# Modulation products: 32 equal moving columns in place of dummy matmuls between their chunks

## The chip, the cores and the metric

The kernel runs on one core of one Trainium2 chip, in one launch. The metric is device microseconds of a run. A core has five engines that run side by side and wait for one another through semaphores: TensorE (PE, matmuls; PEld are its weight loads), VectorE (DVE), ScalarE (ACT), GpSimd (POOL) and SyncE (SP, which issues most of the DMAs).

## The reference

A transformer block for 2048 tokens of width 512, with adaptive layer norm. A condition vector `c` gives six vectors of 512 values, which shift, scale and gate the two halves of the block; all tensors are bfloat16.

```
mod = silu(c) @ w_mod                      # (1, 512) @ (512, 6*512)
sa, ca, ga, sb, cb, gb = six slices of mod
h = layernorm(x) * (1 + ca) + sa
x = x + ga * attention(h)                  # 32 query heads, 8 key/value heads of 128,
                                           # the last 512 cached positions, softmax, wo
h = layernorm(x) * (1 + cb) + sb
x = x + gb * (relu(h @ w1) @ w2)           # 512 -> 1792 -> 512
```

## The kernel before

The program is written as one list of operations for each engine, in the order in which the Python code calls `kb.op`. Every engine runs its list strictly in that order; `kb.op` works out from the declared reads and writes which semaphores each operation waits for. So the order of the calls is the order on the engine, and nothing is reordered later.

The 2048 tokens are cut into 4 blocks of 512 (`QB`), and a block into 4 tiles of 128. Block and head make a unit; there are 128 units. For a unit the kernel computes Q (`q_mms`, 4 matmuls of 512 columns), the scores (`s_mms`, 4 of 512), their exponentials on ScalarE, the product with V (`pv_mms`, 16 of 129) and, spread between units as background work, the output projection. The two layers of the feed-forward part stand at the end. In that long stretch TensorE's queue is full.

The change lies ahead of the first unit, in the start of the kernel, where several short chains have to meet:

- **Loads.** `x` of block 0 comes in two DMAs; then `c`; then the first two slices of `w_mod`, which hold `sa` and `ca`, in four DMAs, one for each chunk of 128 input rows (`load_wm01`, chunks 0 and 2 issued by ScalarE, 1 and 3 by SyncE); then the first heads of `wq`, and K and V.
- **The condition vector.** It is transposed by TensorE (line 1418), and ScalarE and VectorE make `silu(c)` of it, in bfloat16, as `sc_bf` (line 1425), one column for each chunk.
- **The modulation products** (`mod_cols_mm`). `sa` and `ca` are wanted with the feature in the partition. So the weights are the stationary operand: for each of 4 chunks `cc`, 2 slices and 4 groups of 128 features, one matmul with 128x128 weights and one moving column `sc_bf[:, cc]`. These 32 matmuls add up eight columns in one PSUM bank (`psQ`). Each chunk waits for its own DMA. `mod_cols_evac` (line 1440, VectorE) then adds 0 or 1 and writes `modc`.
- **The layer norm of block 0.** VectorE makes the statistics of tiles 0 to 2 (`ln_stat`) and normalises them (`ln_norm`, line 1395); ScalarE does tile 3. TensorE transposes each tile in four 128x128 pieces (`ln_tposes`, line 1377). Tiles 0 and 1 go into banks of `psS`, tiles 2 and 3 into banks of `psO` and `psW`.
- **The modulated input.** VectorE and ScalarE scale and shift the transposes with `modc` into `hT` (`mod_half`, lines 1641 and 1643), in two halves of 256 tokens. Then Q of the first heads follows (`q_half`).

`warm(n)` puts n dummy matmuls into TensorE's list: 512 columns of ones against weights of ones, into a PSUM bank whose content nobody reads. They stand in several places of the start: ten at the very beginning, three and two behind statistics of tiles, one between each two chunks' modulation products, three behind the transposes of tiles 0 and 1, and one behind those of tiles 2 and 3. All matmuls go through `mm`, so line 1374 is that of nearly every one; in the profile they are told apart by their operands: `psW<-ones`, `psO<-ones` and `psS<-ones` are dummies, `psQ<-sc_bf,wmw` are the modulation products, `psS<-ident,xn` and `psO<-ident,xn` the transposes.

VectorE's list in that stretch reads: statistics of tile 2, normalisation of tiles 0 and 1, the addition of `mod_cols_evac`, normalisation of tile 2, `mod_half` for two chunks of the first half, then the second half.

Of the kernel before, what the change touches and what calls it, by code (L numbers as in the profile page):

```python
# [9 lines left out]
ALU = mybir.AluOpType  # L10
# [127 lines left out]
def build_general(nc, es, A_x, A_k_cache, A_v_cache, A_wq, A_wo, B_x, B_w1, B_w2, c, w_mod, out, cfg=None):  # L138
# [27 lines left out]

    NQT = cfg.get("NQT", 4)
    NPB = cfg.get("NPB", 4)
# [11 lines left out]
    if True:  # L180
# [4 lines left out]
        def AL(name, n):  # L185
            lay[name] = (off[0], n)
            off[0] += n + (n % 2)
# [8 lines left out]
        AL("U", max(DC * 6 * D + G * KC * Dh, NOT * QB))  # L196
        AL("qT", NQT * QB)
        AL("Pb", NPB * pslot)
# [36 lines left out]
        def ring(name, n, sz):  # L235
            o = lay[name][0]
            return [arena[:, o + i * sz: o + (i + 1) * sz] for i in range(n)]
# [22 lines left out]
        oT = [arena[:, Ub + i * QB: Ub + (i + 1) * QB] for i in range(NOT)]  # L260
        qT = ring("qT", NQT, QB)
        Pb = ring("Pb", NPB, pslot)
# [66 lines left out]
        R_w2 = RL("w2", FC)  # L329
        R_qT = RL("qT", NQT)  # L330
        R_Pb = RL("Pb", NPB)
# [497 lines left out]
        def rec_qp(i, k):  # L829
# [11 lines left out]
            if k == DC - 1:  # L841
                qs = i % NQT
                if LN1_FOLD:
# [6 lines left out]
        def rec_qk(i, tl):  # L850
            b, h = units[i]
            g = h // R
            qs = i % NQT
            pbs = i % NPB
# [344 lines left out]
def build_fast(nc, es, top, A_x, A_k_cache, A_v_cache, A_wq, A_wo, B_x, B_w1, B_w2, c, w_mod, out, flag):  # L1199
    P = 128  # L1200
# [11 lines left out]
    DC = D // P  # L1212
# [10 lines left out]
    NPT = 3  # L1223
    NOS = 4
    NQT = 3
    VW = P + 8

    def T(name, shape, dt=BF):
        return es.enter_context(nc.sbuf_tensor(name, shape, dt))
# [6 lines left out]
    kT_sb = T("kT", [P, G, W])  # L1236
    v_sb = T("v", [P, G, KC, VW])
    hT = [T(f"hT{i}", [P, DC, QB]) for i in range(2)]
# [8 lines left out]
    wm = [wm01[:, :, 0:D], wm01[:, :, D:2 * D]] + [wmw[:, i * DC * D:(i + 1) * DC * D].rearrange("p (c n) -> p c n", c=DC) for i in range(2, 6)]  # L1247
# [12 lines left out]
    m01 = T("m01", [P, 2 * DC], F32)  # L1260
    sc_bf = T("sc_bf", [P, DC])
    sc_f = T("sc_f", [P, DC], F32)
    tmp = T("tmp", [P, DC], F32)
    modc = T("modc", [P, 4 * DC], F32)
# [17 lines left out]
    bank = [s_ps[0][:, 0, :], s_ps[0][:, 1, :], s_ps[1][:, 0, :], s_ps[1][:, 1, :], q_ps[:, :],  # L1282
            o_ps[:, 0:2, :].rearrange("p a b -> p (a b)"), o_ps[:, 2:4, :].rearrange("p a b -> p (a b)"), w_ps[:, :]]
# [3 lines left out]
    kb = KB(nc)  # L1287
    PE = kb.stream("pe", sem("s_pe"))
    ACT = kb.stream("act", sem("s_act"))
    DVE = kb.stream("dve", sem("s_dve"))  # L1290
# [22 lines left out]
    R_b = RL("bank", 8)  # L1313
# [9 lines left out]
    R_cf, R_m01 = Res("cf"), Res("m01")  # L1323
# [32 lines left out]
    def wm_res(sl, cc):  # L1356
        return R_wmc[cc] if sl < 2 else R_wm[sl]
# [15 lines left out]
    def mm(out_ap, lhsT, rhs, start, stop, reads, bk, signal):  # L1373
        kb.op(PE, lambda e: e.matmul(out_ap, lhsT, rhs, start=start, stop=stop), reads=reads, group_writes=[R_b[k] for k in bk], signal=signal)  # L1374
# [4 lines left out]
    def warm(n, gate=(), bk=7):  # L1379
        for i in range(n):  # L1380
            mm(bank[bk], ones[:, :], ones[:, 0:1].to_broadcast([P, QB]), True, True, [R_ones] + list(gate), [bk], i == n - 1)
# [25 lines left out]
    def ln_tposes(tl, bks):  # L1407
        for cc in range(DC):
            bk = bks[cc]
            o = TO[tl // 2][cc] + tl % 2 * P  # L1410
            tpose(bank[bk].bitcast(BF)[:, o:o + P], xn[:, tl, cc * P:(cc + 1) * P], [R_xn[tl]], [bk], cc == DC - 1)
# [15 lines left out]
    def mod_cols_mm(which, bk):  # L1427
        fs = []
        for cc in range(DC):
            for sl in (0, 1):  # L1430
                for c2 in range(DC):
                    last = sl == 1 and c2 == DC - 1 and cc == DC - 1
                    fs.append(lambda sl=sl, c2=c2, cc=cc, col=sl * DC + c2, last=last: mm(
                        bank[bk][:, col:col + 1], wm[sl][:, cc, c2 * P:(c2 + 1) * P], sc_bf[:, cc:cc + 1],
                        cc == 0 and sl == 0 and c2 == 0, last, [R_sc, wm_res(sl, cc)], [bk], last))
        return fs

    def mod_cols_evac(which, bk):
        mo, r = which * 2 * DC, (R_moda, R_modb)[which]
        kb.op(DVE, lambda e: e.tensor_tensor(modc[:, mo:mo + 2 * DC], bank[bk][:, :2 * DC], m01[:, :], op=ALU.add), reads=[R_b[bk], R_m01], writes=[r])  # L1440

    def mod_part(sl, cc):
        dst, r = pr[sl - 2], R_pr[sl - 2]
# [135 lines left out]
    kb.op(POOL, lambda e: e.memset(cst[:, 3:4], -1.0), writes=[R_eps])  # L1579
    kb.op(POOL, lambda e: e.memset(v_sb[:, :, :, P:VW], 1.0), writes=[R_v1])  # L1580
    kb.op(POOL, lambda e: e.memset(m01[:, 0:DC], 0.0), writes=[R_m01])
# [13 lines left out]
    def rstd_pow(lo, hi):  # L1595
# [12 lines left out]
          reads=[R_x[t3], R_nmr, R_rstd[t3]], writes=[R_xn[t3]])  # L1608
# [8 lines left out]
    def q_evac_half(u, hf, bk, eng):  # L1617
# [4 lines left out]
        else:  # L1622
            kb.op(ACT, lambda e: e.activation(dst, src, ACTF.Copy), reads=[R_b[bk]], writes=w)

    fs = mod_cols_mm(0, QBK)
    for i, f in enumerate(fs):
        f()
        if i in (7, 15, 23):
            warm(1, bk=6)
    ln_tposes(0, TB[0])  # L1630
    mod_cols_evac(0, QBK)
    HB = QB // 2
    R_half = [R_h0, R_hT[0]]
# [56 lines left out]
    for g in range(G):  # L1690
        for i, op in enumerate((ALU.max, ALU.min)):
            add((3, 5, 12, 16, 20, 24, 28, 32)[g], lambda g=g, i=i, op=op: kb.op(DVE, lambda e: e.tensor_reduce(vmax[:, i, g:g + 1], v_sb[:, g, :, 0:Dh], axis=AX.XY, op=op),
                                                             reads=[R_v[g]], writes=[R_vmax]))
# [139 lines left out]
def bass_adaLN_cond__sliding_block_cached__dense_activation_relu__prompt_kernel(  # L1833
# [14 lines left out]
    with ExitStack() as top:  # L1848
        flag = top.enter_context(nc.sbuf_tensor("flag", [1, 8], mybir.dt.int32))
        with ExitStack() as es:  # L1850
            kb, fast, cut, dma_cnt, flag_ev = build_fast(nc, es, top, *args, flag)
            sems = dict(kb.sems)
            meet = top.enter_context(nc.semaphore("s_meet"))
# [84 lines left out]
```

## Time and profile before

| | |
|---|---|
| median of 3 runs | 563.0 us (562.88 to 563.35) |
| the profiled execution's own time | 563.35 us |
| its span, first to last instruction | 558.9 us |
| TensorE busy, share of the span | 550.6 us, 99% |
| ScalarE busy | 349.7 us, 63% |
| VectorE busy | 255.0 us, 46% |
| first modulation product starts | 7.21 us |
| first transpose of `xn` starts | 8.66 us |
| first Q product starts | 10.42 us |

All times in the profile are microseconds from the start of the span. A row of the timeline gives the start, the time from the start of the first to the end of the last instruction merged into it, the engine, the line, the operation, the tiles (written, then read), the shape and the count. Matmuls are pipelined: a row's length includes the time until its last result is out, so the pitch, the distance between starts, tells what a matmul costs in a row of others. The ends of matmuls are modelled.

### The profile page before, as it was taken

To read this page: it belongs to the slowest core of one execution; us is meant where nothing else is said; L and a number is where in the kernel's file an instruction comes from. 1 tells how busy PE (TensorE), PEld (TensorE's weight loads), DVE (VectorE), ACT (ScalarE), POOL (GpSimd) and SP (SyncE) were. 2 spreads that over 40 slices of the span, in tenths; PEclk is the share of its full clock that TensorE was granted. 3 is DMA by queue.
4 is the path that set the end of the run, shared out by engine and by line. 5 is a ranking of instruction groups with operands and counts; after the bars stand their busy time and mean duration, and the time that the engine had idled before them with its cause. 6 is when DMAs were issued, how large, how long until landed. Compare 5 with 4: busy or idle time off the path is not lost.

```text
span 558.9 us, 9695 instructions
## 1 busy us (share of the span) xinstructions
PE 550.6 (99%) x4070; PEld 317.1 (57%) x4144; DVE 255.0 (46%) x556; ACT 349.7 (63%) x455; POOL 52.7 (9%) x50
## 2 busy tenths in 40 slices
PE   9999999999999999999999999999999999999997
PEld 4665555555555555555555555555555554444444
DVE  5555555553546544335445443333354438322134
ACT  5986666666666666666666666666666644432500
POOL 2000022004500000033000000332000000000000
PEclk9999999999999999999999999999999999999999
DMA  9998772522224244253453321121123210200001
GB/s 250 283 197 187 131 153 56 114 44 72 38 42 72 39 85 105 60 130 58 97 94 56 76 40 39 39 38 39 38 39 76 39 29 0 50 28 21 21 29 48
DMA packets 113356, 42.66 MB, mean 76 GB/s; under 512 B 93976, under 2 KB 112152, under 8 KB 113304
## 3 DMA queue, kind: packets, MB, share of 16 engines
q1 hardware_dynamic: 112584, 41.08, 36.2%
q10 hardware_dynamic: 720, 0.89, 0.5%
q8 instruction: 33, 0.54, 0.4%
q14 instruction: 19, 0.16, 0.1%
HBM read 18.35 MB, written 2.10 MB: 37 GB/s over the span
## 4 chain that ended last, share of the span: by engine, by line
PE 99%; issue 1%; DVE 0%
PE psS L1374 29%; PE psO L1374 27%; PE psQ L1374 23%; PE psW L1374 20%; PE psS L1377 0%; PE psO L1377 0%; DVE PT L1755 0%; DVE PT L1757 0%; DVE ones L1574 0%; PE psO L1418 0%; PE psW L1377 0%
## 5 line engine op out<-in xcount | busy, mean ns | idle before, releaser
L1498 ACT ACTIVATE PT<-psS 128x1024 bf16<-128x1024 f32 x254 | 260.6, 1028 | 127.0 <-PE psS L1374 126.9
L1374 PE MATMUL psS<-qT,kT 128*128 128x512 bf16 (+1 forms) x514 | 151.4, 377 | 0.2
L1374 PEld LDWEIGHTS psO<-v,PT 128*128 128x128 bf16 x2048 | 126.6, 98 | 30.2
L1374 PE MATMUL psO<-v,PT 128*128 128x129 bf16 x2048 | 137.0, 220 | 0.0
L1374 PE MATMUL psQ<-hT,wq 128*128 128x512 bf16 (+1 forms) x505 | 129.2, 377 | 0.2
L1508 DVE RECIPROCAL rinv<-psO 128x4 f32<-128x4 f32 x128 | 23.4, 183 | 225.2 <-PE psO L1374 225.2
L1374 PE MATMUL psW<-wo,oT 128*128 128x512 bf16 x452 | 118.1, 379 | 3.2
L1509 DVE TENSOR_TENSOR o<-psO,rinv 128x512 bf16<-128x512 f32 x128 | 88.5, 691 | 4.7 <-DVE rinv L1508 0.3
L1374 PEld LDWEIGHTS psS<-qT,kT 128*128 128x128 bf16 x516 | 50.0, 98 | 58.7 <-issue 0.4
L1374 PEld LDWEIGHTS psQ<-hT,wq 128*128 128x128 bf16 x508 | 49.7, 98 | 59.0
L1490 ACT ACTIVATE qT<-psQ 128x512 bf16<-128x512 f32 x125 | 74.0, 592 | 0.0
L1744 ACT ACTIVATE wq<-psS 128x512 bf16<-128x512 f32 x56 | 33.4, 597 | 49.1 <-PE psS L1374 49.1
L1374 PEld LDWEIGHTS psW<-wo,oT 128*128 128x128 bf16 x512 | 44.9, 98 | 32.9 <-DVE acc L1531 1.2
L1531 DVE TENSOR_TENSOR acc<-psW,acc 128x512 f32<-128x512 f32 x48 | 33.2, 691 | 6.7 <-PE psW L1374 6.7
L1374 PE MATMUL psO<-wmw,wq 128*128 128x512 bf16 (+1 forms) x165 | 32.8, 352 | 0.2
L1534 POOL TENSOR_TENSOR acc<-acc,gaf 128x512 f32<-128x512 f32 x12 | 15.6, 1300 | 146.7 <-DVE acc L1531 139.8
L1390 POOL TENSOR_TENSOR rstd<-rstd,cst 128x4 f32<-128x4 f32 x7 | 7.2, 1026 | 217.1 <-DVE rstd L1389 217.1
L1755 DVE TENSOR_TENSOR PT<-psO,gbf 128x512 f32<-128x512 f32 (+1 forms) x12 | 7.5, 624 | 40.4 <-PE psO L1374 40.4
L1374 PE MATMUL psS<-h2T,wmw 128*128 128x512 bf16 x110 | 25.2, 379 | 0.1
L1374 PEld LDWEIGHTS psO<-wmw,wq 128*128 128x128 bf16 x168 | 15.4, 98 | 16.5
L1374 PE MATMUL psS<-hT,wmw 128*128 128x512 bf16 x110 | 24.4, 379 | 0.1
L1384 DVE BATCH_NORM_STATS2 st<-x 128x6 f32<-128x512 bf16 x31 | 21.1, 681 | 3.6 <-DMA x<-in_A_x_dram 3.6
(95 smaller groups left out, 199.3 us busy)
## 6 DMA issues: line engine op xcount, KB each, us to landing
wo<-in_A_wo_dram SPq DMA_DIRECT2D x4, 1024.0 KB, 5.9
wq<-in_A_wq_dram SPq DMA_DIRECT2D x7, 512.0 KB, 5.2
wmw<-in_B_w_dram SPq DMA_DIRECT2D x14, 256.0 KB, 3.0
wmw<-in_w_mod_dram SPq DMA_DIRECT2D x4, 512.0 KB, 4.9
oT<-o SPq DMA_TRANSPOSE x128, 2.4
out_dram<-PT SPq DMA_DIRECT2D x15, 128.0 KB, 1.7
x<-in_A_x_dram SPq DMA_DIRECT2D x3, 512.0 KB, 4.2
v<-in_A_v_cache_dram SPq DMA_DIRECT2D x8, 128.0 KB, 4.7
```

The source lines that it names most:

```text
L1374: kb.op(PE, lambda e: e.matmul(out_ap, lhsT, rhs, start=start, stop=stop), reads=reads, group_writes=[R_b[k] for k in bk], signal=signal)
L1384: kb.op(DVE, lambda e: e.bn_stats(st[:, t, :], x_sb[:, t, :]), reads=[R_x[t]], writes=[R_st[t]])
L1390: kb.op(POOL, lambda e: e.tensor_tensor(rstd[:, sl], rstd[:, sl], cst[:, 0:1].to_broadcast([P, hi - lo]), op=ALU.pow), reads=R_rstd[sl] + ...
L1490: kb.op(ACT, lambda e: e.activation(qT[u % NQT][:, :], bank[bk], ACTF.Copy), reads=[R_b[bk]], writes=[R_qT[u % NQT]])
L1498: kb.op(ACT, lambda e: e.activation(PT[u % NPT][:, pr * 2:pr * 2 + 2, :], s_ps[pr][:, :, :], ACTF.Exp, scale=scale), reads=[R_b[pr * 2], R ...
L1508: kb.op(DVE, lambda e: e.reciprocal(rinv[:, u, :], o_ps[:, :, P]), reads=[R_b[5], R_b[6]], writes=[R_rinv])
L1509: kb.op(DVE, lambda e: e.tensor_tensor(o_sb[u % NOS][:, :, :], o_ps[:, :, 0:P], rinv[:, u, :].unsqueeze(2).to_broadcast([P, TPB, P]), op=A ...
L1531: kb.op(DVE, lambda e: e.tensor_tensor(acc[:, tl, :], bank[WBK], acc[:, tl, :], op=ALU.add), reads=[R_b[WBK], R_acc[tl]], writes=[R_acc[tl]])
L1534: kb.op(eng, lambda e: e.tensor_tensor(acc[:, tl, :], acc[:, tl, :], gaf[:, :], op=ALU.mult), reads=[R_acc[tl], R_ga], writes=[R_acc[tl]])
L1744: kb.op(ACT, lambda e: e.activation(h1T[b % 2][:, fc, :], bank[bk], ACTF.Relu), reads=[R_b[bk]], writes=[R_h1[b % 2][fc]], pre=all_events( ...
L1755: kb.op(DVE, lambda e: e.tensor_tensor(yt[i][:, c0:c1], bank[bk][:, c0:c1], gbf[:, c0:c1], op=ALU.mult), reads=[R_b[bk], R_gb], writes=[R_ ...
```

## The change

The modulation products get a moving operand of 32 columns, all equal: the one column of `silu(c)` is read 32 times through a broadcast. Each product then writes 32 equal columns of PSUM, so the eight results lie 32 columns apart, and `mod_cols_evac` reads the first column of each group. The three dummy matmuls between the chunks are taken out. The dummies in the other places stay as they are, three behind the transposes of tiles 0 and 1 and one behind those of tiles 2 and 3. TensorE's list is shorter by these three matmuls and their weight loads; the other engines have the same instructions in the same order.

```diff
+    NR = 32
...
                     fs.append(lambda sl=sl, c2=c2, cc=cc, col=sl * DC + c2, last=last: mm(
-                        bank[bk][:, col:col + 1], wm[sl][:, cc, c2 * P:(c2 + 1) * P], sc_bf[:, cc:cc + 1],
+                        bank[bk][:, col * NR:(col + 1) * NR], wm[sl][:, cc, c2 * P:(c2 + 1) * P], sc_bf[:, cc:cc + 1].to_broadcast([P, NR]),
                         cc == 0 and sl == 0 and c2 == 0, last, [R_sc, wm_res(sl, cc)], [bk], last))
...
     def mod_cols_evac(which, bk):
-        kb.op(DVE, lambda e: e.tensor_tensor(modc[:, mo:mo + 2 * DC], bank[bk][:, :2 * DC], m01[:, :], op=ALU.add), reads=[R_b[bk], R_m01], writes=[r])
+        kb.op(DVE, lambda e: e.tensor_tensor(modc[:, mo:mo + 2 * DC], bank[bk][:, :2 * DC * NR].rearrange("p (c r) -> p c r", r=NR)[:, :, 0], m01[:, :], op=ALU.add), reads=[R_b[bk], R_m01], writes=[r])
...
     fs = mod_cols_mm(0, QBK)
-    for i, f in enumerate(fs):
+    for f in fs:
         f()
-        if i in (7, 15, 23):
-            warm(1, bk=6)
     ln_tposes(0, TB[0])
     mod_cols_evac(0, QBK)
```

## The prediction

> **What bounds the kernel now.** I read the page first, then the chain that ended last, then the first 12 us engine by engine. The page's sections 1 and 4:
>
> ```profile
> PE 550.6 (99%) x4070; PEld 317.1 (57%) x4144; DVE 255.0 (46%) x556; ACT 349.7 (63%) x455; POOL 52.7 (9%) x50
> PE 99%; issue 1%; DVE 0%
> ```
>
> The chain that sets the end is TensorE from start to finish. The waits of TensorE's matmul row hold one entry in the whole execution, 1.1 us before the first matmul. So a microsecond saved or lost on TensorE's path in the first 10 us arrives whole at the end, and nothing later absorbs it. The edit touches only 7.2 to 8.8 us. The chain in order of time, 0 to 20 us, shows that stretch (start, length, what):
>
> ```profile
> 5.67 1.70 PE psW L1374 x5
> 7.37 0.18 PE psQ L1374 x8
> 7.55 0.24 PE psO L1374
> 7.79 0.18 PE psQ L1374 x8
> 7.97 0.24 PE psO L1374
> 8.21 0.18 PE psQ L1374 x8
> 8.38 0.24 PE psO L1374
> 8.62 0.18 PE psQ L1374 x8
> 8.80 0.47 PE psS L1377 x8
> ```
>
> The psQ rows are the modulation products, the psO rows the three dummies that go, psS the transposes. (The chain counts by ends; the timeline's starts lie 0.16 us earlier.) Read alone, it promises 3 x 0.24 = 0.72 us. What the dummies cover has to be read from the weight loads, from VectorE and from the DMAs. Timeline of the weight loads, then of VectorE:
>
> ```profile
> 7.41 0.46 PEld L1374 LDWEIGHTS psQ<-sc_bf,wmw 128*128 128x128 bf16 x8
> 8.02 0.27 PEld L1374 LDWEIGHTS psQ<-sc_bf,wmw 128*128 128x128 bf16 x8
> 8.27 0.45 PEld L1374 LDWEIGHTS psQ<-sc_bf,wmw 128*128 128x128 bf16 x8
> ```
>
> ```profile
> 7.99 0.73 DVE L1395 TENSOR_SCALAR xn<-x,mv,rstd 128x512 bf16<-128x512 bf16 x2
> 8.84 0.17 DVE L1440 TENSOR_TENSOR modc<-psQ,m 128x8 f32<-128x8 f32 x1
> 8.92 0.40 DVE L1395 TENSOR_SCALAR xn<-x,mv,rstd 128x512 bf16<-128x512 bf16 x1
> 9.31 0.41 DVE L1641 TENSOR_SCALAR hT<-psS,modc 128x256 bf16<-128x256 bf16 x1
> ```
>
> And the DMA view, in a window of 0.16 us around the issues of the third and fourth chunk of the modulation weight (queue, size, us to landing):
>
> ```profile
> wmw<-in_w_mod_dram ACTq DMA_DIRECT2D x1, 256.0 KB, 6.3
> wmw<-in_w_mod_dram SPq DMA_DIRECT2D x1, 256.0 KB, 6.2
> ```
>
> By the timeline these two were issued at 1.72 and 2.06 us, so chunk 2 landed at about 8.0 and chunk 3 at 8.2. The same view gives chunk 0 as issued at 1.24 and 4.2 us to landing, chunk 1 as 1.66 and 5.5: landed at 5.4 and 7.1. The weight loads of chunks 2 and 3 start at 8.02 and 8.27, right behind their landings. The dummies at 7.83 and 8.25 (timeline) thus stand largely in time in which TensorE would have waited for its weights.
>
> **The change part by part.** *Three dummies out.* Each has a pitch of 0.21 us (7.41 to 7.63, 7.83 to 8.04, 8.25 to 8.46), 0.64 us in all, and that is the most this part can give. *32 columns for one in 32 products.* The one-column row has a pitch of 25 ns (eight from 7.21 to 7.41). The transposes, 128 columns each, run at 56 ns (8.66 to 8.72, 8.72 to 8.77), a 512-column dummy at 216 ns (6.99 to 7.21). The line through the last two gives 0.417 ns a column and 2.7 ns fixed, hence 16 ns for 32 columns, below the 25 ns row. So 25 ns it is, the nearest row in length; the other end is 56 ns.
>
> With 25 ns, chunk 0 runs 7.21 to 7.41, chunk 1 (landed at 7.1) 7.41 to 7.61. Then TensorE waits for chunk 2: 8.04 to 8.24, and for chunk 3: 8.29 to 8.49. Before, the products ended at 8.66. So 0.17 us remain of 0.64; the DMAs take the rest. Behind the waiting products in TensorE's queue stand the transposes. Those of tile 0 need its normalised rows, done at about 8.40 (7.99 plus 0.41), so they go at 8.49. Those of tile 1 need rows that VectorE ends at 8.72 (7.99 plus 0.73). Weight loads followed their releaser by 0.06 us elsewhere (sc_bf ends at 7.06, load at 7.12), so load at 8.78 and first transpose near 8.80, against 8.88 before. That is 0.08 us, and it is what the path gains: after them come three dummies, the transposes of tiles 2 and 3, one dummy and the first Q products, back to back from 9.10 to 10.42, and each moves up by as much. The next releasers do not object: the addition on line 1440 goes from 8.84 to about 8.67, the normalisation of tile 2 behind it to 8.75, ending at 9.15, and its transposes are due at 9.68.
>
> *The strided read on line 1440.* Eight values, 32 columns apart, in place of eight adjacent ones: 0.17 us if the count sets it (the one row; its neighbours of 1 to 8 values take 0.15 to 0.18), 0.42 if the 256 columns spanned did (the 256-column read of line 1621). I take 0.17. With 0.42 the normalisation of tile 2 would end at 9.40, still before 9.68; the first scaling of hT on line 1641 would start 0.1 us later, its cover being the 10.42 start of Q.
>
> Nothing else moves. Order on the other engines is unchanged; no DMA is issued elsewhere; in place of the dummies TensorE gets the exposed wait for chunk 2, 0.41 us.
>
> *What the array is fed.* [...] The page's PEclk says 9 in every slice, also the first, so the clock must be read from pitches. From 1.10 to 6.47 the 512-column dummies come 0.43 us apart, then 0.30, then 0.22: half speed until about 6.6 us and full speed ever since. [...] From 6.77 to 10.42 us the array was fed 9 dummies x 512 + 16 transposes x 128 + 32 = 6,688 columns, at 0.42 ns 2.8 of 3.65 us, 77%. Afterwards it is 6 x 512 + 2,048 + 1,024 = 6,144 columns, 2.6 of 3.57 us, 72%. In the products' own stretch it falls from 0.66 of 1.45 us (45%) to 0.43 of 1.28 (34%), with a hole of 0.41 us in it. [...]
>
> [...]
>
> The sum: -0.08 us, between -0.17 (tile 1 no limit) and, at 56 ns a product, 4 x 0.45 us from 7.21 = 9.01, so +0.35. This execution took 563.35 us: a span of 558.9 and 4.45 around it. It would become 563.27; the median of the runs, 563.0, lies 0.35 below, so 562.9. The gain is 0.01%; a measurement of this kernel can tell about 0.2%, 1.1 us, from no change.
>
> **The rivals.** [...]
>
> *The products are the path (faster).* If the landings come earlier in most executions and VectorE's rows too, the 0.64 us come through: 562.35, still within 0.2%. The weight loads at 8.02 and 8.27 speak against it. Nothing in the profile offers the 1.1 us that a measurable gain needs; I leave it what the trace may not show, such as a profiled execution with landings unlike the others'.
>
> *A 32-column product costs as much as a 128-column one.* Then +0.35: 563.35, also within 0.2%. The edit would not do what it says, being dearer than the dummies it replaces. The line through the longer rows speaks against it.
>
> **How the numbers follow.** No change to be measured: 0.51, made up of the forecast (0.36), the products as path (0.07) and the dear products (0.08); its own range is 562.3 to 563.7 with the runs' scatter (562.88 to 563.35). Clock falls: 0.41, most of it between 564.1 and 564.9; above that lies 0.11. Faster by over 0.2%: 0.08. The likeliest case gives 562.9. The range runs from 562.3 to 564.9, leaving out the faster case and the long half-speed stretches, about 2 in 10.
>
> **What would show it.** Right: no dummy rows between the psQ rows; psQ at 25 ns; weight loads of chunks 2 and 3 again near 8.0 and 8.25; the transposes of tile 1 near 8.80; Q's first product near 10.34; pitches of 216 ns for 512 columns all through. Wrong in the clock: pitches of 0.43 us for 512 columns, or 0.21 for 256, somewhere after 8 us. Wrong in the size: psQ at 56 ns, or weight loads of chunk 2 well before 8.0.

## The result, and the profile after

The changed kernel takes 560.97 us (median of 6 runs, 560.93 to 561.68), the kernel before 563.04 (562.88 to 563.56): a ratio of 0.9965, with a 95% interval of 0.9953 to 0.9978. It is 2.1 us faster, outside the predicted range of 562.3 to 564.9.

The profiled execution does not show these 2 us. Its span is 558.7 us, 0.2 below that of before. Page of the changed kernel, head and sections 1 and 4:

```profile
span 558.7 us, 9689 instructions
PE 549.4 (98%) x4067; PEld 316.4 (57%) x4141; DVE 255.1 (46%) x556; ACT 349.7 (63%) x455; POOL 52.8 (9%) x50
PE 97%; issue 1%; DVE 1%; DMA 1%
```

The chain in order of time now leaves TensorE ahead of the transposes: their releaser is VectorE's normalisation (xn), as TensorE was through with the products by then.

```profile
8.08 0.33 DVE xn L1396
8.41 0.05 issue
8.46 0.72 PE psS L1378 x8
```

Weight loads, VectorE, and the first Q products, from the timeline:

```profile
7.12 0.99 PEld L1375 LDWEIGHTS psQ<-sc_bf,wmw 128*128 128x128 bf16 x32 [0.57 <-DVE sc_bf L1426]
8.64 0.16 DVE L1441 TENSOR_TENSOR modc<-psQ,m 128x8 f32<-128x8 f32 x1
8.84 0.41 DVE L1396 TENSOR_SCALAR xn<-x,mv,rstd 128x512 bf16<-128x512 bf16 x1
10.33 0.60 PE L1375 MATMUL psQ<-hT,wq 128*128 128x256 bf16 x4
```

The 32 products run almost in one piece. The first Q product starts at 10.33, 0.09 us before the 10.42 of the kernel before; the span is 0.2 us shorter. Neither difference between these two executions is clear of the scatter: in eight profiled executions of what the kernel before executes (its own and those of the experiments below), the first Q product starts anywhere from 10.02 to 11.08 us. The landings of chunks 2 and 3 (DMA view around their issues) were earlier than in the other execution:

```profile
wmw<-in_w_mod_dram ACTq DMA_DIRECT2D x1, 256.0 KB, 5.9
wmw<-in_w_mod_dram SPq DMA_DIRECT2D x1, 256.0 KB, 5.7
```

Where, then, are the 2 us? In the table of before stood two numbers side by side: the execution's own time, 563.35, and its span, 558.9. Between them lie 4.45 us. In the profiled execution of the changed kernel it is 561.68 and 558.7: 2.98. (It is the slowest of the six; their median outside the span is 2.3.) By definition no instruction is recorded behind the span, but DMAs are. The DMA view from 557 to 565 us, in 40 slices of 0.2 us; first the kernel before:

```profile
GB/s 8 12 6 13 149 3 0 0 0 0 82 0 0 0 0 0 0 0 0 0 0 0 0 0 0 0 0 0 0 0 41 0 0 0 0 0 0 0 0 0
q8 instruction: 1, 0.02, 1.1%
q14 instruction: 1, 0.01, 0.4%
```

and the changed kernel:

```profile
GB/s 12 6 20 142 1 0 0 0 0 82 0 0 0 0 0 0 41 0 0 0 0 0 41 0 0 0 0 0 0 0 0 0 0 0 0 0 0 0 0 0
q8 instruction: 1, 0.02, 1.0%
q14 instruction: 2, 0.02, 0.7%
```

The profile names the kind of queues 8 and 14 "instruction"; I read their transfers as fetches of program code. A slice with 82 GB/s holds one of 16,384 bytes (queue 8), one with 41 GB/s one of 8,192 (queue 14). Both kernels fetch 16 KB in the slices at 559.0 and 558.8, just behind the span. But the last 8 KB start at 563.0 before and at 561.4 after. This fits engines that still have code to run when the span is over, and that took longer over it before the change. The fetch of 8 KB is no exact mark of the end, though: in the run with two matmuls fewer below it lies in the slice from 560.2 to 560.4, and that execution still took 561.61 us.

By its amount I take queue 8 for TensorE's: section 3 of the page before gives it 0.54 MB in 33 fetches, for 8,214 recorded TensorE instructions. That is about 66 bytes each, some 250 instructions to a fetch; I count with 256, an estimate. The three dummies with their weight loads are six instructions, and the heads of the pages differ by six (9695 and 9689). Behind TensorE's last matmul the program jumps over the fallback path (a second version of the whole kernel, run only if a flag says so) to the code that ends it. The jump is a row of the profile of before:

```profile
L1878 PEldq COMPARE_BRANCH  x2: 90/1878/3666, 509.9 to 554.6; - x2
```

Of the two branches on this line, the first, at 509.9, takes 0.09 us; the second, at 554.6, is the jump. It takes 3.67 us, until 558.3, and queue 8 fetches 16 KB during it. In the changed kernel it takes 3.55 us. So the jump itself is hardly different and lies inside the span; but by this estimate six instructions fewer move the end code to another place in a block of fetched code.

### The profile page after: what moved, and what is told of

Same layout as the page of the kernel before. It is cut to its first block, busy times and chain, and to the rows that moved or that the text cites. A ratio compares the mean times of both kernels' runs of the same rounds, so it can differ in the third digit from the quotient of the medians.

```text
span 558.7 us, 9689 instructions
## 1 busy us (share of the span) xinstructions
PE 549.4 (98%) x4067; PEld 316.4 (57%) x4141; DVE 255.1 (46%) x556; ACT 349.7 (63%) x455; POOL 52.8 (9%) x50
## 4 chain that ended last, share of the span: by engine, by line
PE 97%; issue 1%; DVE 1%; DMA 1%
PE psS L1375 29%; PE psO L1375 27%; PE psQ L1375 22%; PE psW L1375 19%; DMA x<-in_A_x_dram 1%; DVE st L1385 0%; PE psS L1378 0%; DVE mv L1386 0%; PE psO L1378 0%; DVE xn L1396 0%; DVE rstd L1594 0%; DVE PT L1754 0%; DVE PT L1756 0%; DVE tmp L1425 0%; DVE sc_bf L1426 0%
```

## The experiments

Theory A: the time hangs on where TensorE's end code lies, hence on the length of its program, not on what the edit does at 7 to 9 us. Rival B: the executed edit brings it. The fallback is never executed for these inputs, so its length can be changed without any effect on the executed instructions. The first two runs use this edit with 3 and with -3:

```diff
+def resize(stream, n):        # n matmuls more, or fewer, in the middle of the fallback
+    ...
                 def rerun():
...
+                    if name == "pe":
+                        resize(general[name], FALLBACK)
                     gkb.emit(general[name], e)
```

**The changed kernel at the old length** (`FALLBACK = 3`).

> The changed kernel, with three matmuls more in the fallback path of TensorE's program, which is not executed for these inputs. TensorE's program is then as long as that of the kernel before; what is executed is that of the changed kernel. Theory A (the 2 us lie outside the span and hang on the length of TensorE's program): span 558.7 us, time back at about 563.0 us. Rival B (the executed edit itself brings the 2 us): span 558.7, time stays at about 561.0 us.

Measured: 563.14 us (ratio 0.9999, 0.9989 to 1.0009), median span 559.0, outside it 4.15. The gain is gone, with the whole edit in place.

**The kernel before at the new length** (`FALLBACK = -3`).

> The kernel before, with three matmuls fewer in the fallback path of TensorE's program, which is not executed for these inputs (the fallback thus lacks three matmuls). TensorE's program is then as long as that of the changed kernel; what is executed is that of the kernel before. Theory A: span 558.9 us as before, time down to about 561.1 us. Rival B: time stays at about 563.0 us.

Measured: 561.51 us (0.9968, 0.9955 to 0.9980), span 558.75, outside 2.7. Most of the gain, with nothing of the edit. Rival B falls with these two.

**32 columns, dummies kept.**

```diff
-                        bank[bk][:, col:col + 1], wm[sl][:, cc, c2 * P:(c2 + 1) * P], sc_bf[:, cc:cc + 1],
+                        bank[bk][:, col * NR:(col + 1) * NR], wm[sl][:, cc, c2 * P:(c2 + 1) * P], sc_bf[:, cc:cc + 1].to_broadcast([P, NR]),
```

(and the strided read on line 1440)

> The kernel before with 32 equal moving columns, the three dummies between the chunks kept. TensorE's program is as long as before. Theory A: 563.0 us, span within 0.1 us of 558.9. Rival B, if the 32 columns bring it: about 561 us.

Measured: 563.13 us (0.9999, 0.9990 to 1.0009). The columns bring nothing and cost nothing that can be measured.

**No dummies, one column.**

```diff
-    for i, f in enumerate(fs):
+    for f in fs:
         f()
-        if i in (7, 15, 23):
-            warm(1, bk=6)
```

> The kernel before without the three dummies, products with one moving column. TensorE's program is as long as that of the changed kernel. Theory A: about 561.0 us, span 558.8, if the clock holds; if the array, fed 5,152 instead of 6,688 columns between 6.8 and 10.4 us, loses full speed, the span grows by about 1.4 us and the time is about 562.4 us. Rival B, if the dummies bring it: 561 us as well; this run tells the columns from the dummies only together with the first two.

Measured: 561.40 us (0.9965, 0.9950 to 0.9979), span 559.0, outside 2.4. The time is that of the shorter program. This run is also the one in which the array is fed least between 6.8 and 10.4 us. Timeline:

```profile
7.48 1.40 PE L1374 MATMUL psQ<-sc_bf,wmw 128*128 128x1 bf16 x32
8.74 0.61 PE L1377 MATMUL psS<-ident,xn 128*128 128x128 bf16 x8
10.50 0.60 PE L1374 MATMUL psQ<-hT,wq 128*128 128x256 bf16 x4
```

Eight transposes in 0.61 us and four matmuls of 256 columns in 0.60 us, as in the kernel before from 8.66 and from 10.42 us on: no speed was lost, after 1.2 us that held nothing but one-column products.

**One and two matmuls fewer** (the kernel before, `FALLBACK = -1` and `-2`).

> The kernel before with one matmul fewer in the unexecuted fallback path of TensorE's program (the fallback lacks it). Theory A, refined: TensorE's last instructions, behind the fallback, straddle the edge of a block of fetched program, and the time outside the span (about 4.2 us before, about 2.4 after the change) goes by steps with their place. Each matmul is two instructions. Either 563.0 us (edge not yet passed) or 561.2 us (passed); nothing in between. Rival (the tail shrinks in proportion to the program's length): about 562.4 us.

> As the run before it, two matmuls fewer. Theory A: 563.0 or 561.2 us, and 561.2 if one fewer gave 561.2. Rival (proportion): about 561.8 us.

Measured: 562.45 us (0.9989, 0.9978 to 0.9999) and 561.73 (0.9980, 0.9970 to 0.9991), outside the span 3.4 and 2.9. These are the rival's numbers, not mine: there is no single step, but between this length and six instructions fewer 0.1 to 0.4 us for each instruction.

**192 and 256 instructions more** (the changed kernel; fulfilled waits behind the fallback, counted as two to an instruction, which no run shows).

```diff
                     gkb.emit(general[name], e)
+                    if name == "pe":
+                        for _ in range(384):      # 512 in the second
+                            e.wait_ge(meet, 1)
```

> The changed kernel with 192 instructions more behind the fallback path of TensorE's program, semaphore waits that are fulfilled at once and are not executed for these inputs. The fetches of TensorE's queue have 16,384 bytes; if an instruction has 64 bytes, that is 256 instructions, and 192 more have the same place in a block as 64 fewer. Theory A: the end code lies wholly inside one block, the time is 561.0 us or less, down to about 559.5 if the second fetch behind the span is not waited for any more. Rival (length in itself): 563 us or more.

> As the run before it with 256 instructions, one whole block. Theory A: same place in the block, same time as the changed kernel, 561.0 us. Rival (length in itself): 563 us or more.

Measured with 192: 560.65 us (0.9959, 0.9945 to 0.9974), outside 1.8. With a longer program the kernel is faster, so length as such is not it. With 256: 561.82 us (0.9982, 0.9972 to 0.9993), outside 3.1. It comes down most of the way, but not to the 2.3 of the changed kernel; it lies where two to four instructions fewer than before lie. The repeat after 256 is thus not exact by my count. Whether the added waits take a few places more than counted, or the block is not quite what I take it for, stays open.

The DMA view of the run with 192, 557 to 565 us, shows the end closer behind the fetch:

```profile
GB/s 14 154 19 3 0 0 0 0 0 0 82 0 0 0 0 0 41 0 0 0 0 0 0 0 0 0 0 0 0 0 0 0 0 0 0 0 0 0 0 0
```

The 16 KB are fetched at 559.0 as before, but the execution ends soon behind them: it took 560.51 us, whereas the kernel before needed almost three more. So that fetch alone is not what costs the time.

**4, 16 and 186 instructions more** (the kernel before, the same edit with 8, 32 and 372 waits).

> The kernel before with 4 instructions more behind the fallback. Theory A: four more instructions of the end code fall behind the edge. If these still belong to what follows the span, the time rises by 4 x 0.3 to about 564.2 us; if they belong to the barrier that ends the span, the second fetch is waited for inside the span, which grows by up to 1.4 us, and the time outside falls by as much: 563.0 us. Rival (before is the worst place by chance, the next step up is a new block): 561 us.

> The kernel before with 16 instructions more behind the unexecuted fallback of TensorE's program (fulfilled semaphore waits). Theory A, as the runs so far leave it: behind the span TensorE needs a second fetch of 16 KB, done near 560.3 us, and what is left of its end code behind the edge of that block costs about 0.3 us an instruction (2.8 us before, 1.5 with six instructions fewer, 0.1 with the end code wholly inside a block). Pushed 16 places on, the end code lies wholly behind the edge, in the block that the jump itself fetches: about 560.7 us. Rival (a longer program costs in proportion, 0.3 us an instruction): about 567 us; a milder rival (the edge only moves into the barrier): 563 us or more.

> The kernel before, executed stream and all, with 186 instructions more behind the fallback: the same place in the block as the changed kernel with 192 more, which took 560.65 us. Theory A: 560.7 us, with the three dummies and the one-column products in place. Rival B (part of that time is owed to the executed edit): 561 us or more.

Measured: 560.49 us (0.9963, 0.9948 to 0.9978), 560.70 (0.9971, 0.9958 to 0.9984) and 560.73 (0.9963, 0.9951 to 0.9975), outside the span 1.8 each. The last two are as theory A had it. The first is a miss: of the three cases the rival's came true. The kernel before stands, by chance, on nearly the worst place, and four instructions further it is over.

**The jump taken away.** TensorE's fallback goes ahead of its last part, as on the other engines, so that no jump lies behind the last matmul.

```diff
-                if name == "pe":
-                    with e.If(v == 128):
-                        last_part()
-                    with e.Else():
-                        rerun()
-                else:
-                    with e.If(v != 128):
-                        rerun()
-                    with e.Else():
-                        last_part()
+                with e.If(v != 128):
+                    rerun()
+                with e.Else():
+                    last_part()
```

> The kernel before with TensorE's two paths in the other order, the fallback first and the last part behind it, so that no jump stands between the last matmul and the end code; the jump now stands in front of the last part, in the feed-forward stretch. Theory A: the time outside the span falls from 4.1 us to 1.8 or less; the span grows by what TensorE loses at the jump, between 0 (if its queue holds enough matmuls) and about 2 us. Time 560.7 to 562.7 us. Rival (the jump is not the cause): time outside the span stays at 4.1 us.

Measured: 560.68 us (0.9965, 0.9950 to 0.9980), span 558.7, outside 2.0. The DMA view, 557 to 565 us:

```profile
GB/s 0 0 90 75 0 0 0 0 0 0 0 0 0 0 0 0 41 0 0 0 0 0 0 0 0 0 0 0 0 0 0 0 0 0 0 0 0 0 0 0
q14 instruction: 1, 0.01, 0.3%
```

Queue 8 fetches nothing behind the span any more. The jump, now in the feed-forward stretch, takes as long as at the end, 3.54 us, but most of it is covered. First its row and the timeline of TensorE there in this run, then the timeline in the kernel before:

```profile
L1877 PEldq COMPARE_BRANCH  x1: 3540/3540/3540, 509.8 to 509.8; - x1
507.07 6.21 PE L1374 MATMUL psO<-wmw,wq 128*128 128x512 bf16 x27
513.40 2.98 PE L1374 MATMUL psQ<-wmw,wq 128*128 128x512 bf16 x13
513.40 2.49 PEld L1374 LDWEIGHTS psQ<-wmw,wq 128*128 128x128 bf16 x13 [0.62 <-issue]
```

```profile
507.15 6.21 PE L1374 MATMUL psO<-wmw,wq 128*128 128x512 bf16 x27
513.20 3.18 PE L1374 MATMUL psQ<-wmw,wq 128*128 128x512 bf16 x14
```

From the first psO to the first psQ it is 6.33 us instead of 6.05, so TensorE loses 0.28 us at the jump. The span hardly shows it (a median of 558.7, with 558.5 of the kernel before in the same set of runs): in the profiled execution the last three output DMAs land 1.5 to 1.6 us after their issue, in that of before 2.0 to 2.8; why, no run here separates. The edit only changes the order of the two paths, so the end code should stand where it stood in the kernel before.

All runs by the length of TensorE's program, in instructions against the kernel before by my count (medians; "outside" is the time less the span of the same run; the kernel before, measured anew with each set of runs, took 563.07, 562.99 and 562.63 us, with 4.25, 4.1 and 4.1 outside):

| TensorE's program | kernels | outside the span, us | time, us |
|---|---|---|---|
| +250 | the changed one | 3.1 | 561.82 |
| +186 | before; the changed one (+192 to itself) | 1.8; 1.8 | 560.73; 560.65 |
| +16 | before | 1.8 | 560.70 |
| +4 | before | 1.8 | 560.49 |
| 0 | before; the changed one; columns only | 4.25; 4.15; 4.0 | 563.07; 563.14; 563.13 |
| -2 | before | 3.4 | 562.45 |
| -4 | before | 2.9 | 561.73 |
| -6 | the changed one; before; no dummies | 2.3; 2.7; 2.4 | 560.97; 561.51; 561.40 |
| no jump | before | 2.0 | 560.68 |

Within one row the times agree within their intervals, whatever the kernel does between 7 and 9 us. Six kernels stand at 560.5 to 561.0, four of them without the edit. So the versions that beat both kernels are those at +4, +16 and +186 and the one without the jump; against the changed kernel they gain 0.2 to 0.5 us at most, which their intervals do not separate.

What is shown: that the number of instructions in TensorE's program decides, though neither more nor fewer is better in itself, and not what is executed; and that at the length of the kernel before the long end goes with the jump over the fallback. Without the jump this one length alone was run. What is argued, and shown by no run: that it is the place in a block of fetched code. The jump does not tell good lengths from bad ones: it takes 3.4 to 3.8 us in all 13 kernels that end with it, 3.67 in the kernel before and 3.73 with four instructions more. And a fetch of 16 KB behind the span is there with 4.25 us outside as with 1.8. The code that runs behind the span is not in the profile, so why an instruction there costs 0.1 to 0.4 us stays open, as does the repeat after 256.

## Why the prediction was wrong

**The step that failed** is the last one of the sum, "a span of 558.9 and 4.45 around it. It would become 563.27", with "Nothing else moves" ahead of it. I held the 4.45 us for a constant. It went to 2.98 in the profiled execution, and in the medians of the runs from 4.25 to 2.3. The removal of three matmuls was priced by what they execute, 0.64 us; that they also take up six places in TensorE's program was not priced, and this was nearly the whole result, 1.9 of 2.1 us. The rest lies in the spans, 558.9 and 558.65 us, and is within their scatter.

**The term inside the span** had the right limit, but its size is not shown. Predicted were -0.08 us, Q at 10.34 and the transposes of tile 1 near 8.80. Measured were Q at 10.33 and eight transposes from 8.46 on, of which the fifth, the first of tile 1, starts at 8.78. The limit was VectorE's rows, as predicted: in all four profiled executions of what the changed kernel executes, Q starts 2.33 us after VectorE begins to normalise tiles 0 and 1 (from 8.00 to 10.33 in two of them, from 7.95 to 10.28 and from 8.11 to 10.44 in the others). In the eight executions of what the kernel before executes it is 2.35 to 2.43 us in four, which makes the gain 0.02 to 0.1 us, and 2.67 to 3.29 in the other four, where the weights were late or the products were the path. The 0.09 between the two profiled executions agrees with the predicted 0.08 in part by luck, since Q also started at 10.33 in two executions with the dummies in place. At equal program length the gain can't be measured (0.9999, 0.9989 to 1.0009).

**The wait for the weights comes and goes.** I had the products wait for chunks 2 and 3 until 8.04 and 8.29. In the changed kernel's execution they had landed by 7.6 and 7.8, so the products of chunk 2 started at 7.65, 0.13 us behind the last of chunk 1 where a wait of 0.41 was predicted, and the products were through before the normalised rows were there. This is one of the signs that the prediction named for being wrong in the size, weight loads of chunk 2 well before 8.0; the path was not touched by it, as VectorE's rows were the later. In the run of the kernel before at the new length the weights were late, and the timeline shows it:

```profile
8.27 0.35 PE L1382 MATMUL psQ<-sc_bf,wmw 128*128 128x1 bf16 x8 [0.27 <-DMA wmw<-in_w_mod_dram]
11.07 0.60 PE L1382 MATMUL psQ<-hT,wq 128*128 128x256 bf16 x4
```

Q at 11.07, and a span of 559.2. The same happened in two more executions of the kernel before (Q at 10.94 and 11.08). The rival in which the products are the path (0.07) also occurs: in the run without the jump, VectorE had the rows of tiles 0 and 1 ready by 8.4, and the transposes came at 8.58, behind the last product. What the edit would gain in such an execution no run shows.

**32 columns at 25 ns** was right: in the run with 192 instructions more, 32 products take 0.95 us with 0.18 for one, which makes 25 ns from start to start. In the changed kernel's own execution they take 1.09 us, 25 ns apart but for a gap of 0.13 us between chunks 1 and 2. The strided read on line 1440 took 0.16 us, where 0.17 was taken.

**The falling clock** (0.41) did not come true in the executions that were profiled. With 5,152 columns of feed between 6.8 and 10.4 us, against 6,688 before, the first four Q products of 256 columns took 0.44 us to the next row (10.50 to 10.94), as in the kernel before (10.42 to 10.86). The holes in the changed kernel's execution, 0.8 us before the first statistics were there and 0.2 us at the transposes, cost no speed: the 512-column dummies behind the first come 0.23 and 0.21 us apart, and the first four Q products behind the second take 0.43 us to the next row (10.33 to 10.76). In place of a fall the runs show these pitches, and no run shows what brings this clock up or takes it down: the 0.41 and its 564.1 to 564.9 us were my estimate, as were the 1.4 us in the expectation for the run without dummies, a quarter of the 5.5 us (1.10 to 6.6) that the pitch of a 512-column dummy took to come down from 0.43 to 0.22 us in the execution of before. That length rested on one execution too: in the changed kernel's it was some 2.7 us, as the dummies load their weights 0.43 us apart until 3.64 us and 0.31 us apart then.

**"Faster by over 0.2%" had 0.08**, as nothing in the profile offered 1.1 us. In the span nothing did. The 4.45 us beside it were there to be read, but with nothing that said by how much they would move.

## What to carry to other kernels

Compare the time with the span of the same execution before pricing anything: what lies between them is also time, and here it was 1.8 to 4.25 us by the length of TensorE's program. If an edit changes the number of instructions and moves the time by a microsecond or two that the timeline does not show, restore the program's length with code that is not executed and measure again. Look for a jump over a long unexecuted block at the very end of an engine's program: with the order of the two paths turned round, the kernel before reached 560.68 us without any edit to its work. Four unexecuted instructions more gave the same, 560.49, but the kernel before, four instructions shorter, took 562.63 us in the same set of runs, so such a place can be lost with the next edit that changes the length.

## What the runs showed of the hardware

- The time outside the recorded span was 1.8 to 4.25 us (medians) by the number of instructions in TensorE's program alone. From the length of the kernel before, each two instructions fewer took off 0.2 to 0.9 us, while four more took off 2.3 at once.
- TensorE's jump over the unexecuted fallback took 3.4 to 3.8 us in 13 kernels at the end (3.67 in the kernel before, 3.55 in the changed one) and 3.54 us in the middle of the feed-forward stretch, where queued matmuls covered all but 0.28 us of it.
- In the kernel before, queue 8, of the kind "instruction", moved 0.54 MB in 33 transfers of 16,384 bytes, about 66 bytes for each recorded TensorE instruction; queue 14, of the same kind, moved 0.16 MB in 19 transfers of 8,192 bytes.
- The 256 KB DMAs of chunks 2 and 3 landed 5.5 and 5.6 us after their issue in the run with 192 instructions more, 6.3 and 6.2 in the kernel before, 6.7 and 6.9 in the kernel before at the new length. Where they were late, TensorE's whole list moved with them: with the first Q product at 10.42 and 11.07 us in two executions of the same work, the last row of matmuls started at 554.01 and 554.66. The spans were 558.9 and 559.2, as the end behind it took 0.3 us less.
